# Attention and a feed-forward layer on one core: blocks of four pairs, grouped attention matmuls, three rooms for q and k, and one list scheduler for the whole program

## The chip, the core and the metric

The kernel runs on one core of a Trainium2 chip. Its time is the device time of one execution in microseconds (us), and the median of several runs is compared. The engines of the core work side by side: TensorE (PE in the profile) multiplies matrices, VectorE (DVE), ScalarE (ACT) and GpSimd (POOL) work on elements, and SyncE (SP) issues the DMA transfers. PEld is PE's loading of the stationary operand.

## The reference, cut to what matters

Attention runs inside chunks of 64 tokens, 8 heads of 64 columns; its output, as 4608 rows of 512 columns, goes through two linear layers with a squared ReLU between them.

```python
scores = scale * np.matmul(q_c, k_c.transpose(0, 1, 2, 4, 3))   # chunks of 64
attn = np.exp(scores - np.max(scores, axis=-1, keepdims=True))
attn = attn / (np.sum(attn, axis=-1, keepdims=True) + 1e-09)
out = np.matmul(attn, v_c)
x = out.transpose(0, 2, 1, 3).reshape(4608, 512)
h = x @ w_in                      # 512 -> 2048
g = np.maximum(h, 0.0) ** 2
return g @ w_out                  # 2048 -> 512
```

## The kernel before

Two chunks are a **pair** of 128 tokens; there are 36. Pairs are gathered into **blocks**, `blocks = [4] + [3] * 10 + [2]`. A block goes through the feed-forward part in 16 steps `f`, each for 128 of the 2048 middle columns. A step multiplies into `h` (`mm_in`, L623: a 128x128 piece of `w_in` stands in the array and the tokens of the block move through it, so a matmul has 128 columns for each pair of the block) and later out of `g` into `o` (`mm_out`, L667: the 128 tokens of one pair stand in the array and 512 columns of `w_out` move). The `o` sums stay in PSUM for all 16 steps, one bank for each pair of the block out of four; `outs` of a step come `LAG = 2` steps behind its `ins`.

Each fp32 operand is split into a high part and the remainder, both in the format in which PE multiplies; a product is three matmuls (high-high, high-low, low-high). A step thus has 12 `h` matmuls, and 3 `o` matmuls for each pair. Between them `Step` does ReLU (L634, ACT), the square (L638 on DVE from block 2 on, L640 on ACT ahead of that), the high part of `g` (L647, ACT) and the low part (L650, DVE).

Attention of the first eight pairs (`Pair`) runs in and ahead of block 0. The other 28 are worked as 56 **units** of four heads, each one slot of the stream behind the other: `stack_qk` transposes and splits q and k (DVE, ACT, and DMAs from one half of the partitions to the other), `s2` makes the scores (L353, four matmuls of 256 columns) and their softmax up to the exponential, `norm` divides (POOL, L390), `s3` transposes the result (L403, two of 128 columns) and stacks it as `pst` (L417, L419, L421), `s4` multiplies with v (L437, four of 256 columns) and writes the tokens `x` of a later block. The raw q and k have tiles of their own, the transposed ones too, and the low part of q has another.

What sets the order: in block 0 a planner (`Plan`) lists all engines' work by costs written into it and issues it in that order. From block 1 on only PE's order is written by hand: `merge` spreads the units' steps one by one, evenly, between the matmuls of the block. The other engines are ordered by the framework's scheduler, with `Step.act` and the stores ahead by a priority. `store` (L680) copies an `o` bank to one of two `ob` tiles (L677 on DVE, L679 on ACT) and issues its DMA.

Of the kernel before, what the change touches and what calls it, by code (L numbers as in the profile page):

```python
# [10 lines left out]
F32 = mybir.dt.float32  # L11
# [9 lines left out]
def kernel(  # L21
# [20 lines left out]
    nc = tc.nc  # L42
# [19 lines left out]
    PRIO = 300  # L62
    blocks = [4] + [3] * 10 + [2]
    LAG = 2
    HEAD = 1
    REST = 0
# [10 lines left out]
    NN = sum(blocks[:2]) + 1  # L77
# [12 lines left out]
    raw = ctx.enter_context(tc.tile_pool(name="raw", bufs=1))  # L90

# [18 lines left out]
    def open_late():  # L110

        early.close()
        pool = ctx.enter_context(tc.tile_pool(name="late", bufs=2))
        late["pool"] = pool
        late["q"] = pool.tile([P, H, 2, CH], F32R, name="qst", tag="qst", bufs=1)
        late["p"] = pool.tile([P, 2, HP, 2, 2, CH], F32R, name="pst", tag="pst", bufs=1)
        load_v(NN)
# [97 lines left out]
    ust = [dict() for _ in units]  # L215
# [27 lines left out]
    def load_qk(pair):  # L243


        pairs[pair] = {}
        for nm, src in (("q", q), ("k", k)):
            t = raw.tile([P, H, IH, 32], F32, name=f"{nm}_raw{pair}", tag=f"{nm}_raw")
            pairs[pair][nm] = t
            for c in range(2):  # L250
                bb, n0 = divmod(2 * pair + c, NCH)
                for dh in range(DH):
                    r0 = c * D + dh * 32
                    for ih in range(IH):
                        i0 = n0 * CH + ih * 32
                        s = src[bb, :, i0:i0 + 32, dh * 32:(dh + 1) * 32]
                        nc.sync.dma_start(out=t[r0:r0 + 32, :, ih, :], in_=s.rearrange("h i d -> i h d"))  # L257

    def load_v(pair):


        if pair < NN:
            for c in range(2):
                bb, n0 = divmod(2 * pair + c, NCH)
                for h2, r in enumerate(halves):
                    s = v[bb, h2:H:2, n0 * CH:(n0 + 1) * CH, :]
                    nc.sync.dma_start(  # L267
                        out=vbd[slot_of(pair)][r, :, c, h2, :], in_=s.rearrange("h i d -> i h d")
                    )
            return  # L270
        pairs[pair]["v"] = []
        for c in range(2):
            t = late["pool"].tile([P, H, D], F32, name=f"v_raw{pair}_{c}", tag="v_raw")
            pairs[pair]["v"].append(t)
            bb, n0 = divmod(2 * pair + c, NCH)
            s = v[bb, :, n0 * CH:(n0 + 1) * CH, :].rearrange("h i d -> i h d")
            for r in halves:
                nc.sync.dma_start(out=t[r], in_=s)

    def transpose_pair(pair):  # L280

        for nm in "qk":
            t = late["pool"].tile([P, H, CH], F32, name=f"{nm}t{pair}", tag=f"{nm}t", bufs=1)
            nc.vector.transpose(
                t.rearrange("p h i -> p (h i)"), pairs[pair][nm].rearrange("p h a d -> p (h a d)")
            )
            pairs[pair][nm] = t
        if pair + 1 < NPAIR:
            load_qk(pair + 1)

    def s1(u):
        b, pair, j, hq = units[u]
        if hq == 0:
            yield lambda: transpose_pair(pair)
            yield lambda: stack_qk(pair)

    def stack_qk(pair):

        qt, kt = pairs[pair]["q"], pairs[pair]["k"]
        kst = late["k"]
        qst = late["q"]
        low = late["pool"].tile([P, H, CH], F32R, name=f"ql{pair}", tag="kk", bufs=1)
        for c, (own, oth) in enumerate(other):
            nc.scalar.copy(qst[own, :, c], qt[own])  # L306
        for c, (own, oth) in enumerate(other):
            nc.vector.tensor_tensor(low[own], qt[own], qst.bitcast(F32)[own, :, c], op=ALU.subtract)
        for c, (own, oth) in enumerate(other):
            nc.sync.dma_start(out=qst.bitcast(F32)[oth, :, c], in_=low.bitcast(F32)[own])  # L310
        for c, (own, oth) in enumerate(other):
            nc.scalar.copy(kst[own, 0, c], kt[own])  # L312
        for c, (own, oth) in enumerate(other):
            nc.sync.dma_start(out=kst.bitcast(F32)[oth, 0, c], in_=kst.bitcast(F32)[own, 0, c])
        for c, (own, oth) in enumerate(other):
            nc.vector.tensor_tensor(
                kst[own, 1, c], kt[own], kst.bitcast(F32)[own, 0, c], op=ALU.subtract
            )

    def split_v(u):  # L320
        yield lambda: stack_v(u)

    def stack_v(u):


        b, pair, j, hq = units[u]
        vs = late["pool"].tile([P, 2, HP, 2, D], F32R, name=f"vs{u}", tag="vs")
        ust[u]["v"] = vs
        for c, t in enumerate(pairs[pair]["v"]):
            vr = t[:, hq * HQ:(hq + 1) * HQ].rearrange("p (a b) d -> p a b d", b=2)  # L330
            nc.scalar.copy(vs[:, c], vr)  # L331
            for h2, r in enumerate(halves):
                dst = (r, slice(None), 1 - h2)
                nc.gpsimd.tensor_tensor(  # L334
                    vs[:, c][dst], vr[dst], vs.bitcast(F32)[:, c][dst], op=ALU.subtract
                )
        if hq == NQ - 1 and pair + 1 < NPAIR:
            load_v(pair + 1)

    def s2(u):  # L340


        st = ust[u]
        b, pair, j, hq = units[u]

        def mm2(h):
            if h % 2 == 0:
                st.setdefault("sc", []).append(
                    bank(("at", next(turn_at) % 2), [P, 2, 2, 2, CH], f"sc{u}_{h}")
                )  # L350
            ps = st["sc"][-1][:, h % 2]
            hh = hq * HQ + h
            nc.tensor.matmul(  # L353
                ps.rearrange("p w c j -> p (w c j)"), late["q"][:, hh].rearrange("p c i -> p (c i)"), late["k"][:, :, :, hh],
                start=True, stop=True,
            )

        def half(h):
            if h == 0:
                st["e"] = late["pool"].tile([P, HQ, CH], F32, name=f"e{u}", tag="e", bufs=2)  # L360
            ps, e = st["sc"][h // 2], st["e"][:, h:h + 2]
            for c, r in enumerate(halves):
                nc.scalar.copy(e[r], ps[r, :, 1, c])  # L363
            for c, r in enumerate(halves):
                nc.vector.tensor_tensor(e[r], ps[r, :, 0, c], e[r], op=ALU.add)  # L365

        def rest():
            e = st["e"]
            m = att.tile([P, HQ, 1], F32, name=f"m{u}", tag="m", bufs=2)
            z = att.tile([P, HQ, 1], F32, name=f"z{u}", tag="z", bufs=2)  # L370
            nc.vector.tensor_reduce(m, e, axis=AX.X, op=ALU.max)
            nc.vector.tensor_tensor(e, e, m.broadcast_to([P, HQ, CH]), op=ALU.subtract)
            nc.scalar.activation(e, e, AF.Exp, scale=QSCALE)
            st["e"] = (e, z)

        for h in range(HQ):
            yield lambda h=h: mm2(h)
            if h % 2:
                yield lambda h=h: half(h - 1)
        yield rest  # L380

    def norm(u):
        st = ust[u]

        def f():
            e, z = st["e"]
            nc.vector.tensor_reduce(z, e, axis=AX.X, op=ALU.add)
            nc.vector.tensor_scalar_add(z, z, 1e-9)
            nc.vector.reciprocal(z, z)
            nc.gpsimd.tensor_tensor(e, e, z.broadcast_to([P, HQ, CH]), op=ALU.mult)  # L390
            st["p"] = e

        yield f

    def s3(u):

        st = ust[u]

        def tr(hp):
            if hp == 0:  # L400
                st["pt"] = bank(("at", next(turn_at) % 2), [P, HP, 2, CH], f"pt{u}")
            ps = st["pt"]
            nc.tensor.transpose(  # L403
                ps[:, hp].rearrange("p a b -> p (a b)"),
                st["p"][:, 2 * hp:2 * hp + 2].rearrange("p a b -> p (a b)"),
                ident,
            )

        for hp in range(HP):
            yield lambda hp=hp: tr(hp)  # L410

        def evac2():
            ps = st["pt"]
# [576 lines left out]
```

## Time and profile before

| | |
|---|---|
| time, median of 3 runs | 938.81 us (937.74 to 940.42) |
| profiled execution: span; the median above it | 936.7 us; 2.1 us |
| PE busy in it | 922.2 us (98%) |
| DVE, ACT, POOL busy | 691.0, 599.6, 211.1 us |
| h matmuls (L623) | 2304: 192 of 512 columns, 1920 of 384, 192 of 256 |
| o matmuls (L667) | 1728 of 512 columns |

The profiled execution's own time is that span and what lies around it outside the trace: the timed runs end 1.0 to 3.7 us above the span, the median 2.1 us above it. Busy time counts an engine's instructions; a busy PE can still be slower than it could be, since a matmul's time is what the next one waits for.

### The profile page before, as it was taken

The page shows a single profiled execution, that of the slowest core. Times are in us where ns is not written, and L with a number is a line of the kernel's source. Part 1 is how long each engine was busy: PE and PEld are TensorE (multiplying, and loading weights), DVE is VectorE, ACT ScalarE, POOL GpSimd, SP SyncE. Part 2 cuts the span into 40 slices and gives each one's busy share as a digit, 9 for nine tenths or more (in the row PEclk, how much of TensorE's full clock was granted, in tenths as well). Part 3 has the DMA queues.
Part 4 walks back from the last instruction along what each step waited for, and adds up shares of the span by engine and source line. Part 5 has one row for each costly group of instructions (what it writes and reads, how often), then busy time and mean ns, then how long its engine had stood idle before and what let it go on. Part 6 is the DMA issues. An engine that isn't in the chain of part 4 may idle for free.

```text
span 936.7 us, 16742 instructions
## 1 busy us (share of the span) xinstructions
PE 922.2 (98%) x5018; PEld 827.8 (88%) x5018; DVE 691.0 (74%) x1591; ACT 599.6 (64%) x1479; POOL 211.1 (23%) x351
## 2 busy tenths in 40 slices
PE   9899999999999999999999999999999999999998
PEld 8788888888899999999999999999999999998997
DVE  5999994678778877877877877877877877753332
ACT  5788876687666666766766766766766666653332
POOL 2000002043222233333322222333333222221000
PEclk9899999999999999999999999999999999999999
DMA  8946425445444543543433533444543442210000
GB/s 185 278 136 209 168 39 118 81 83 104 96 79 78 112 77 75 112 76 74 106 70 72 112 72 69 110 76 79 113 80 75 89 103 57 57 40 12 1 35 23
DMA packets 287193, 85.01 MB, mean 91 GB/s; under 512 B 268672, under 2 KB 276864, under 8 KB 287104
## 3 DMA queue, kind: packets, MB, share of 16 engines
q1 hardware_dynamic: 284992, 83.42, 40.7%
q8 instruction: 41, 0.67, 0.3%
q10 hardware_dynamic: 2112, 0.52, 0.3%
q14 instruction: 48, 0.39, 0.1%
HBM read 52.43 MB, written 9.44 MB: 66 GB/s over the span
## 4 chain that ended last, share of the span: by engine, by line
PE 90%; DVE 3%; ACT 2%; DMA 1%; SPq 1%; issue 1%; POOL 1%; ACTq 0%; DVEq 0%; POOLq 0%
PE h L623 41%; PE o L667 40%; PE sc L353 3%; PE xt L437 3%; PE pt L403 1%; PE xt L581 1%; PE sc L527 1%; DMA wiraw<-in_moe_w_in_dram 1%; SPq L257 0%; SPq L267 0%; ACT qst L306 0%; ACT kst L312 0%; POOL vbd L800 0%; DVE wia L177 0%; DMA kst<-kst 0%
## 5 line engine op out<-in xcount | busy, mean ns | idle before, releaser
L623 PE MATMUL h<-xh,wi 128*128 128x384 f32 (+2 forms) x1536 | 433.4, 339 | 0.2 <-DVE wi L198 0.2
L667 PE MATMUL o<-wo,gh 128*128 128x512 f32 x1152 | 372.0, 397 | 0.6 <-ACT ob L679 0.6
L623 PEld LDWEIGHTS h<-xh,wi 128*128 128x128 f32 x1536 | 274.9, 188 | 14.2 <-DVE wi L198 0.8
L623 PE MATMUL h<-xl,wi 128*128 128x384 f32 (+2 forms) x768 | 260.5, 339 | 0.2 <-DVE xl L594 0.2
L667 PEld LDWEIGHTS o<-wo,gh 128*128 128x128 f32 x1152 | 207.9, 188 | 33.7 <-ACT ob L679 1.0
L667 PE MATMUL o<-wo,gl 128*128 128x512 f32 x576 | 226.5, 393 | 0.0
L334 POOL TENSOR_TENSOR vs<-v_raw,vs 64x128 fp32r<-64x128 f32 x224 | 114.7, 512 | 238.8 <-ACT vs L331 218.8
L650 DVE TENSOR_TENSOR gl<-g,gh 128x384 fp32r<-128x384 f32 (+2 forms) x192 | 111.4, 580 | 68.8 <-ACT gh L647 64.8
L623 PEld LDWEIGHTS h<-xl,wi 128*128 128x128 f32 x768 | 144.6, 188 | 7.3 <-DVE xl L594 0.5
L634 ACT ACTIVATE g<-h 128x384 f32<-128x384 f32 (+2 forms) x192 | 94.5, 492 | 79.4 <-PE h L623 59.2
L647 ACT CAST gh<-g 128x384 fp32r<-128x384 f32 (+2 forms) x192 | 98.5, 513 | 71.0 <-PE o L667 53.3
L638 DVE TENSOR_TENSOR g<-g 128x384 f32<-128x384 f32 (+1 forms) x160 | 88.9, 556 | 64.1 <-ACT g L634 62.7
L667 PEld LDWEIGHTS o<-wo,gl 128*128 128x128 f32 x576 | 108.2, 188 | 20.7
L390 POOL TENSOR_TENSOR e<-e,z 128x256 f32<-128x256 f32 x56 | 45.3, 810 | 233.1 <-PE o L667 69.7
L365 DVE TENSOR_TENSOR e<-sc,e 64x128 f32<-64x128 f32 x224 | 64.7, 289 | 36.7 <-ACT e L363 31.4
L363 ACT COPY e<-sc 64x128 f32<-64x128 f32 x224 | 58.2, 260 | 43.1 <-PE sc L353 40.2
L451 DVE TENSOR_TENSOR x<-xt,x 64x128 f32<-64x128 f32 x224 | 64.6, 289 | 22.7 <-ACT x L449 18.5
L449 ACT COPY x<-xt 64x128 f32<-64x128 f32 x224 | 58.0, 259 | 35.2 <-PE xt L437 31.9
L353 PE MATMUL sc<-kst,qst 128*128 128x256 f32 x224 | 62.8, 281 | 2.0 <-DVE pst L421 1.2
L437 PE MATMUL xt<-pst,vs 128*128 128x256 f32 x224 | 62.6, 280 | 2.1 <-DMA pst<-pst 2.1
L457 POOL TENSOR_TENSOR xl<-x,xh 128x256 fp32r<-128x256 f32 x56 | 44.3, 790 | 59.5 <-ACT xh L456 57.1
L421 DVE TENSOR_TENSOR pst<-pt,pst 64x256 fp32r<-64x256 f32 x112 | 47.3, 422 | 10.9 <-ACT pst L417 6.9
(80 smaller groups left out, 912.4 us busy)
## 6 DMA issues: line engine op xcount, KB each, us to landing
v_raw<-in_v_dram SPq DMA_DIRECT2D x112, 128.0 KB, 3.3
out_dram<-ob SPq DMA_DIRECT2D x36, 256.0 KB, 2.1
wiraw<-in_moe_w_in_dram SPq DMA_DIRECT2D x16, 512.0 KB, 6.2
woraw<-in_moe_w_out_dram SPq DMA_DIRECT2D x16, 512.0 KB, 6.0
q_raw<-in_q_dram SPq DMA_DIRECT2D x224, 32.0 KB, 2.1
k_raw<-in_k_dram SPq DMA_DIRECT2D x224, 32.0 KB, 2.1
qst<-ql SPq DMA_DIRECT2D x56, 128.0 KB, 2.6
kst<-kst SPq DMA_DIRECT2D x56, 128.0 KB, 2.6
```

The costliest lines, as they stand in the source:

```text
L334: nc.gpsimd.tensor_tensor(vs[:, c][dst], vr[dst], vs.bitcast(F32)[:, c][dst], op=ALU.subtract)
L353: nc.tensor.matmul(ps.rearrange("p w c j -> p (w c j)"), late["q"][:, hh].rearrange("p c i -> p (c i)"), late["k"][:, :, :, hh], start=Tru ...
L363: nc.scalar.copy(e[r], ps[r, :, 1, c])
L365: nc.vector.tensor_tensor(e[r], ps[r, :, 0, c], e[r], op=ALU.add)
L437: nc.tensor.matmul(st["xt"][hp][:, c].rearrange("p w a q -> p (w a q)"), st["v"][:, c, hp].rearrange("p a d -> p (a d)"), late["p"][:, :, ...
L451: nc.vector.tensor_tensor(x[r, hp], ps[hp][r, :, 0, h2], x[r, hp], op=ALU.add)
L623: nc.tensor.matmul(self.h[:, :self.n], a[:, c], bb[:, c, :self.n], start=c == 0 and i == 0, stop=c == NCC - 1 and i == 2,)
L634: nc.scalar.activation(self.g, self.h[:, :self.n], AF.Relu)
L638: nc.vector.tensor_tensor(self.g, self.g, self.g, op=ALU.mult)
L647: nc.scalar.copy(self.gh[:, :self.n], self.g)
L650: nc.vector.tensor_tensor(self.gl[:, :self.n], self.g, self.gh.bitcast(F32)[:, :self.n], op=ALU.subtract)
L667: nc.tensor.matmul(acc[b, j], a[:, j * P:(j + 1) * P], bb, start=f == 0 and i == 0, stop=f == NF - 1 and i == 2,)
```

## The change

Blocks become nine of four pairs, so every `h` matmul has 512 columns. Each unit's work is cut into methods of one instruction each (class `Unit`), and the planner, which now knows a cost for every one of them, lists all engines of the whole program. PE's order stays fixed by a token that its work shares; the others go by what is ready first, then by a due time counted backwards. The attention of a unit no longer goes singly between matmuls but in three bunches in each slot, at 0, 0.31 and 0.62 of it. Raw and transposed q and k share a ring of three tiles, and the low part of q is written over the transposed q. The first late pair's raw q and k go into the two `ob` tiles, before any `ob` needs them. The square goes to DVE in even steps and to ACT in odd ones. The copy and the store of `o` are two operations now. The eight early pairs (`NN`) and all instructions of a unit stay.

```diff
-    blocks = [4] + [3] * 10 + [2]
+    blocks = [4] * 9
-    NN = sum(blocks[:2]) + 1
+    NN = sum(blocks[:2])
+        ring.extend(pool.tile([P, H * CH], F32, name=f"ring{n}", tag=f"ring{n}", bufs=1) for n in range(3))
...
+    def room(pair, n):
+        if pair == NN and n < 2:
+            return gp.tile([P, DM], F32, name=f"{'qk'[n]}_raw{pair}", tag="o")
+        return ring[(4 * (pair - NN) + n) % 3]
...
+            self.on_vector = b > 0 and f % 2 == 0
...
         def square(self):
-            if self.b > 1:
+            if self.on_vector:
...
-        HOP = 0.2
+        HOP = {PE: 0.27, DVE: 0.07, ACT: 0.07, POOL: 0.1, SP: 0.1}
...
+            for n in reversed(range(len(ops))):
+                engine, cost, _, _, size, rank = ops[n]
+                if size:
+                    cost += size / self.RATE + self.LATENCY
+                due[n] = min((due[x] - self.hop(n, x) for x in after[n]), default=self.END) - cost
+                if rank is not None:
+                    due[n] = rank
...
+                    key = (max(free.get(ops[n][0], 0.0), ready[n]), due[n], n)
...
+    SPOTS = (0.0, 0.31, 0.62)
+    LEAD = 0.06
...
+        def pe(cost, fn, reads, writes):
+            add(PE, cost, fn, reads, [*writes, "pe"])
...
+                if s.f == NF - 1:
+                    ob = ("ob", next(stores) % 2)
+                    add(DVE if j % 2 else ACT, TWO if j % 2 else ONE, lambda j=j: s.keep(j), [o], [ob])
+                    add(SP, ISSUE, lambda j=j: s.store(j), [ob], size=256 * KB)
...
+        def slot(t):
+            r = []
+            for at_, stages in zip(SPOTS, (((3, values),), ((2, turn), (2, split_v)), ((1, scores), (0, begin)))):
+                r.append((at_, [lambda st=st, un=unit[t - lag]: st(un) for lag, st in stages if NQ * NN <= t - lag < NU]))
+            return r
...
+        if not last:
+            n0 = NQ * first_pair[b + 1] + 3 if b > 1 else NQ * NN + 1
+            n1 = NQ * (first_pair[b + 1] + blocks[b + 1])
+            slots = [slot(t) for t in range(n0, n1 + 3)]
+        spread(ops, slots, LEAD if b == 1 else 0.0)
```

The first place is PE in the middle of a block, from step 5 to step 6 (`sc` are a unit's score matmuls, `xt` those with v). Before, they stand one at a time between matmuls of 384 and 512 columns:

```order
L623 MATMUL h_5_4708<-xh_3517,wi_768 128x384
L667 MATMUL o_0_4547<-wo_723,gh_3_4619 128x512 x2
L353 MATMUL sc_2_4737<-kst,qst 128x256
L667 MATMUL o_0_4547<-wo_723,gl_3_4620 128x512
L667 MATMUL o_1_4552<-wo_723,gh_3_4619 128x512 x2
L667 MATMUL o_1_4552<-wo_723,gl_3_4620 128x512
L353 MATMUL sc_2_4737<-kst,qst 128x256
L667 MATMUL o_2_4561<-wo_723,gh_3_4619 128x512 x2
L667 MATMUL o_2_4561<-wo_723,gl_3_4620 128x512
L623 MATMUL h_6_4758<-xh_3517,wi_821 128x384
```

Of the change, the same engine and steps:

```order
L598 MATMUL h_5_5458<-xh_4002,wi_778 128x512
L343 MATMUL sc_0_5478<-kst,qst 128x256 x2
L343 MATMUL sc_2_5481<-kst,qst 128x256 x2
L598 MATMUL h_5_5458<-xh_4002,wi_778 128x512
L598 MATMUL h_5_5458<-xl_4003,wi_778 128x512
L598 MATMUL h_5_5458<-xh_4002,wi_778 128x512
L635 MATMUL o_0_5279<-wo_738,gh_3_5417 128x512 x2
L635 MATMUL o_0_5279<-wo_738,gl_3_5418 128x512
L635 MATMUL o_1_5288<-wo_738,gh_3_5417 128x512 x2
L635 MATMUL o_1_5288<-wo_738,gl_3_5418 128x512
```

The four score matmuls moved together, the four with v do the same (eight rows further on), and all that stands between the bunches has 512 columns.

The second place is SP in block 0, where the raw q and k of the last two of the eight early pairs are loaded (`qk_raw`), with `vbd` the tile of v for one of them, which waits until PE is done with the one that it held. Before:

```order
L241 DMA qk_raw_504<-in_q_dram 128x4x64 x2
L241 DMA qk_raw_504<-in_k_dram 128x4x64 x2
L267 DMA vbd_89<-in_v_dram 64x4x64 x4
L146 DMA woraw_819<-in_moe_w_out_dram 128x1024
L144 DMA wiraw_824<-in_moe_w_in_dram 128x4x256
```

Of the change:

```order
L235 DMA qk_raw_501<-in_q_dram 128x4x64 x2
L235 DMA qk_raw_501<-in_k_dram 128x4x64 x2
L257 DMA q_raw_529<-in_q_dram 32x8x32 x8
L257 DMA k_raw_576<-in_k_dram 32x8x32 x8
L265 DMA vbd_86<-in_v_dram 64x4x64 x4
L141 DMA woraw_830<-in_moe_w_out_dram 128x1024
L139 DMA wiraw_834<-in_moe_w_in_dram 128x4x256
```

The 16 loads of the first late pair moved ahead of the `vbd` loads and of all weight loads behind them.

## Rows read from the trace of the kernel before

**Rows 1.** The page: span and busy time of each engine.

```profile
span 936.7 us, 16742 instructions
PE 922.2 (98%) x5018; PEld 827.8 (88%) x5018; DVE 691.0 (74%) x1591; ACT 599.6 (64%) x1479; POOL 211.1 (23%) x351
```

**Rows 2.** Windows: busy PE, PEld, DVE, ACT, POOL (instructions), PE clock, DMA, GB/s.

```profile
146.00:245.00 99.00, 94.40 (x496) 83.72 (x495) 68.42 (x163) 68.88 (x176) 25.45 (x45) 1.00 0.50 102
421.25:495.00 73.75, 73.75 (x397) 66.99 (x397) 58.27 (x141) 48.99 (x130) 21.83 (x36) 1.00 0.43 87
```

**Rows 3.** PE's waits, 146 us to the end: total us, times, longest.

```profile
PE xt L437 <- DMA pst<-pst: 2.1, 2, 1.3
PE pt L403 <- DVE x L451: 1.3, 1, 1.3
PE sc L353 <- DVE pst L421: 1.2, 3, 0.7
PE sc L353 <- DMA kst<-kst: 0.7, 1, 0.7
PE o L667 <- ACT ob L679: 0.6, 1, 0.6
```

**Rows 4.** Pieces of the chain: start, us, engine, tile, line, instructions.

```profile
49.81 2.72 PE h L623 x12
54.26 2.82 PE o L667 x12
59.80 2.04 PE o L667 x9
...
365.10 2.10 PE h L623 x12
413.62 2.08 PE o L667 x9
...
883.91 1.43 PE h L623 x12
```

**Rows 5.** Timeline of PE behind transposes of block 0.

```profile
40.54 0.39 PE L623 MATMUL h<-xl,wi 128*128 128x512 f32 x1
...
41.70 0.60 PE L503 MATMUL k<-ident,qk_raw 128*128 128x128 f32 x4
```

**Rows 6.** Groups of the page: busy us, mean ns, idle before them.

```profile
L390 POOL TENSOR_TENSOR e<-e,z 128x256 f32<-128x256 f32 x56 | 45.3, 810 | 233.1 <-PE o L667 69.7
L365 DVE TENSOR_TENSOR e<-sc,e 64x128 f32<-64x128 f32 x224 | 64.7, 289 | 36.7 <-ACT e L363 31.4
L363 ACT COPY e<-sc 64x128 f32<-64x128 f32 x224 | 58.2, 260 | 43.1 <-PE sc L353 40.2
```

**Rows 7.** DVE's groups by shape (columns as in rows 6).

```profile
L650 DVE TENSOR_TENSOR gl<-g,gh 128x384 fp32r<-128x384 f32 x160 | 93.6, 585 | 56.2 <-ACT gh L647 52.5 <-PE o L667 1.9
L638 DVE TENSOR_TENSOR g<-g 128x384 f32<-128x384 f32 x144 | 82.1, 570 | 44.7 <-ACT g L634 43.3
L650 DVE TENSOR_TENSOR gl<-g,gh 128x512 fp32r<-128x512 f32 x16 | 11.0, 686 | 0.6 <-ACT gh L647 0.3
```

**Rows 8.** SP's timeline in block 0, and eight loads later.

```profile
51.74 3.46 SPq L241 DMA_DIRECT2D qk_raw<-in_k_dram  x2
65.80 2.63 SPq L267 DMA_DIRECT2D vbd<-in_v_dram  x4
...
397.72 4.03 SPq L257 DMA_DIRECT2D k_raw<-in_k_dram  x8
```

**Rows 9.** The end's timeline, ACT's wait for ob, and the page's landing time.

```profile
932.47 0.59 ACT L679 COPY ob<-o 128x512 f32<-128x512 f32 x1 [1.86 <-PE o L667]
933.15 0.69 DVE L677 COPY ob<-o 128x512 f32<-128x512 f32 x1 [2.08 <-PE o L667]
ACT ob L679 <- DMA out_dram<-ob: 9.9, 11, 2.0
out_dram<-ob SPq DMA_DIRECT2D x36, 256.0 KB, 2.1
```

More of the change, by code (lines that the diff above doesn't have):

```diff
@@ L259, in load_v @@
-    def load_v(pair):
[L262 to L271, printed above, removed]
+    ring = []
+    def room(pair, n):
+        if pair == NN and n < 2:
+            return gp.tile([P, DM], F32, name=f"{'qk'[n]}_raw{pair}", tag="o")
+        return ring[(4 * (pair - NN) + n) % 3]
@@ new lines, in load_qk @@
+    def load_qk(pair, n, part):
+        src = (q, k)[n]
+        at = pairs.setdefault(pair, {})
+        if n not in at:
+            at[n] = room(pair, n)
+        t = at[n].rearrange("p (h a d) -> p h a d", h=H, a=IH)
+        c, dh, ih = part
+        bb, n0 = divmod(2 * pair + c, NCH)
+        r0 = c * D + dh * 32
+        i0 = n0 * CH + ih * 32
+        s = src[bb, :, i0:i0 + 32, dh * 32:(dh + 1) * 32]
+        nc.sync.dma_start(out=t[r0:r0 + 32, :, ih, :], in_=s.rearrange("h i d -> i h d"))
@@ L291, in s1 @@
[L291 to L315, printed above, removed]
+            for h2, r in enumerate(halves):
+                s = v[bb, h2:H:2, n0 * CH:(n0 + 1) * CH, :]
+                nc.sync.dma_start(
+                    out=vbd[slot_of(pair)][r, :, c, h2, :], in_=s.rearrange("h i d -> i h d")
+                )
@@ L340, in s2, with raw_v @@
[L340 to L346, printed above, removed]
-            if h % 2 == 0:
[L348 to L352, printed above, removed]
+                late["k"][own, 1, c], pairs[self.pair]["t", 1][own],
+                late["k"].bitcast(F32)[own, 0, c], op=ALU.subtract,
+            )
+        def raw_v(self, c):
+            return pairs[self.pair]["v", c][:, self.heads].rearrange("p (a b) d -> p a b d", b=2)
@@ new lines, in high_v, with low_v, score @@
+        def high_v(self, c):
+            if not c:
+                self.v = late["pool"].tile([P, 2, HP, 2, D], F32R, name=f"vs{self.u}", tag="vs")
+            nc.scalar.copy(self.v[:, c], self.raw_v(c))
+        def low_v(self, c, h2):
+            dst = (halves[h2], slice(None), 1 - h2)
+            nc.gpsimd.tensor_tensor(
+                self.v[:, c][dst], self.raw_v(c)[dst], self.v.bitcast(F32)[:, c][dst], op=ALU.subtract
+            )
+        def score(self, h, which):
+            if h % 2 == 0:
+                self.sc = bank(which, [P, 2, 2, 2, CH], f"sc{self.u}_{h}")
+            ps = self.sc[:, h % 2]
+            hh = self.hq * HQ + h
@@ L380, in s2 @@
[L380 to L402, printed above, removed]
+                ps.rearrange("p w c j -> p (w c j)"), late["q"][:, hh].rearrange("p c i -> p (c i)"),
@@ new lines, in score, with take, join @@
+                late["k"][:, :, :, hh], start=True, stop=True,
+            )
+            if h % 2:
+                self.done = getattr(self, "done", {})
+                self.done[h // 2] = self.sc
+        def take(self, part, c):
+            if not part and not c:
+                self.e = late["pool"].tile([P, HQ, CH], F32, name=f"e{self.u}", tag="e", bufs=2)
+            r = halves[c]
+            nc.scalar.copy(self.e[r, 2 * part:2 * part + 2], self.done[part][r, :, 1, c])
+        def join(self, part, c):
+            r = halves[c]
+            e = self.e[r, 2 * part:2 * part + 2]
+            nc.vector.tensor_tensor(e, self.done[part][r, :, 0, c], e, op=ALU.add)
@@ L425, in s3, with high_p @@
-        yield evac2
-    def s4(u):
-        st = ust[u]
-        b, pair, j, hq = units[u]
-        def mm2(hp, c):
-            if c == 0:
-                st.setdefault("xt", []).append(
-                    bank(("at", next(turn_at) % 2), [P, 2, 2, 2, CH], f"xt{u}_{hp}")
-                )
+                self.pt[:, hp].rearrange("p a b -> p (a b)"),
+                self.e[:, 2 * hp:2 * hp + 2].rearrange("p a b -> p (a b)"), ident,
+            )
+        def high_p(self, h2):
+            own, _ = other[h2]
+            nc.scalar.copy(late["p"][own, 0, :, :, h2], self.pt[own])
@@ new lines, in send_p, with low_p, value @@
+        def send_p(self, h2):
+            own, oth = other[h2]
+            f = late["p"].bitcast(F32)
+            nc.sync.dma_start(out=f[oth, 0, :, :, h2], in_=f[own, 0, :, :, h2])
+        def low_p(self, h2):
+            own, _ = other[h2]
+            nc.vector.tensor_tensor(
+                late["p"][own, 1, :, :, h2], self.pt[own],
+                late["p"].bitcast(F32)[own, 0, :, :, h2], op=ALU.subtract,
+            )
+        def value(self, hp, c, which):
+            if not c:
+                if not hp:
+                    self.xt = []
+                self.xt.append(bank(which, [P, 2, 2, 2, CH], f"xt{self.u}_{hp}"))
@@ L459, in s4, with take_x, join_x @@
-        for hp in range(HP):
-            for c in range(2):
-                yield lambda hp=hp, c=c: mm2(hp, c)
-            yield lambda hp=hp: evac(hp)
+        def take_x(self, hp, h2):
+            if not hp and not h2:
+                self.x = late["pool"].tile([P, HP, 2, CH], F32, name=f"x{self.u}", tag="x", bufs=1)
+            r = halves[h2]
+            nc.scalar.copy(self.x[r, hp], self.xt[hp][r, :, 1, h2])
+        def join_x(self, hp, h2):
+            r = halves[h2]
+            x = self.x[r, hp]
+            nc.vector.tensor_tensor(x, self.xt[hp][r, :, 0, h2], x, op=ALU.add)
@@ L464, in x_of, with place @@
+        def place(self, part):
+            xh, xl = x_of(self.b)
+            dst = (slice(None), slice(self.hq * HP, (self.hq + 1) * HP), slice(self.j * P, (self.j + 1) * P))
+            src = self.x.rearrange("p a c i -> p a (c i)")
+            if part == 0:
+                nc.scalar.copy(xh[dst], src)
+            else:
+                nc.gpsimd.tensor_tensor(xl[dst], src, xh.bitcast(F32)[dst], op=ALU.subtract)
     def x_of(b):
@@ L767, in run @@
                 t, _, n = best
-                engine, cost, _, _, size, _ = ops[n]
-                free[engine] = t + cost
-                end[n] = t + cost
+                engine, cost, fn, _, size, _ = ops[n]
+                end = free[engine] = t + cost
                 if size:
-                    queue = max(queue, t + cost) + size / self.RATE
-                    end[n] = queue + self.LATENCY
+                    queue = max(queue, end) + size / self.RATE
+                    end = queue + self.LATENCY
+                if loads and loads[-1] == n:
+                    loads.pop()
                 order.append((t, n))
-                left.remove(n)
+                open_.remove(n)
+                for x in after[n]:
+                    ready[x] = max(ready[x], end + self.hop(n, x))
+                    waits[x] -= 1
+                    if not waits[x]:
+                        open_.add(x)
+            assert len(order) == len(ops)
             for _, n in sorted(order):
@@ new lines, with spread @@
+    unit = [Unit(u) for u in range(NU)]
+    def spread(ops, slots, start):
+        todo = [((start + (1 - start) * (s + at) / len(slots)) * len(ops), x) for s, groups in enumerate(slots) for at, x in groups]
+        for n, op in enumerate(ops):
+            while todo and todo[0][0] <= n:
+                for x in todo.pop(0)[1]:
+                    x()
+            op()
+        for _, xs in todo:
+            for x in xs:
+                x()
+    with tc.manual_schedule(engines={PE, DVE, ACT, SP, POOL}):
+        program()
```

419 lines of the change are left out of this document (234 added, 185 removed).

## The prediction

> **What bounds the kernel now.** I read the page first: PE is busy 922.2 of 936.7 us, DVE 691.0, ACT 599.6 [rows 1]. That a busy PE is also the one that is waited for must come from a stretch, so the windows came next. In 421 to 495 us, which is exactly one block of three pairs, PE is busy 73.75 of 73.75 us; DVE has 58.27 (79%), ACT 48.99 (66%) [rows 2]. In 146 to 245 us, where the units begin, PE is busy 94.40 of 99.00, so 4.6 us are lost there. The list of PE's waits confirms that there is little else: after 146 us they sum to 5.9 us, five kinds [rows 3]. So the kernel is bounded by the spacing of PE's own matmuls, and the question is what one costs in each shape.
>
> The pieces of the chain give that [rows 4]. Twelve h matmuls of 512 columns take 2.72 us, 226.7 ns each; of 384 columns 2.10 us, 175 ns; of 256 columns 1.43 us, 119 ns. Nine o matmuls, 512 columns, take 2.04 us in block 0 when nothing of another shape stands ahead of them (226.7 ns) and 2.08 us later (231.1 ns), where matmuls of 384 and 256 columns stand among them. In block 0, where all feed-forward matmuls have 512 columns, one piece of twelve behind attention takes 2.82 us. The timeline shows the same directly behind transposes: from 40.54 to 41.70 us five matmuls start, 232 ns each (the first row and the one behind the fifth) [rows 5]. I read this as: a foreign shape disturbs the spacing of the some ten matmuls behind it by about 4.4 ns each (231.1 less 226.7).
>
> A check: a block of three is 192 x 0.175 + 144 x 0.2311 = 66.9 us of h and o; the remaining 6.85 us of 73.75 are six units, 1.14 us a unit on PE.
>
> **The change, part by part.**
>
> *Blocks of four.* Before: h is 192 x 0.2267 + 1920 x 0.175 + 192 x 0.119 = 402.4 us. After: 1728 x 0.2267 = 391.7. The columns are the same in sum; 576 fixed costs go. By the rows that fixed cost is 13 to 15 ns (226.7 less 512 columns at 2.4 GHz is 13.4; 175 less 160 is 15; the granted clock is 1.00 in these windows [rows 2], its level of 2.4 GHz). o before: 192 x 0.2267 in block 0 and 1536 x 0.2311 after it, 398.5 us; after, undisturbed, 391.7. Together 800.9 to 783.4: **-17.5 us**.
>
> On this point a rule speaks against the change. The Trainium skill, "TensorE: Matmul & The Clock Gate", section "Wait — 56ns, not 53.3ns?", gives a fixed cost of about 2.5 ns for a warm matmul; by it 576 fewer matmuls are worth 1.4 us, not the 10.7 us of h. The trace differs, with 13 to 15 ns at three widths, and I go by the trace.
>
> *Attention in bunches.* Each of 56 units has three bunches: 168 places where the shape changes, in blocks 1 to 7. With ten disturbed matmuls behind each, 1680 of the 2688 there cost 4.4 ns more: **+7.4 us**. Nothing in the trace shows these groups between 512-wide matmuls alone. The lower bound is 0 (the 2.04 us piece), the upper one all 3072 matmuls of blocks 1 to 8, 13.5 us (the 2.08 us piece). I take the middle because attention stands nearest to it. The attention matmuls are the same in number and shape, 1.14 us a unit: 0.
>
> *Waits.* A slot in blocks 2 to 7 is (384 x 0.229 + 8 x 1.14) / 8 = 12.1 us. Scores stand at 0.62 of a slot, the transpose at 0.31 of the next: 0.69 x 12.1 = 8.3 us. What must happen between is, by the groups, the second part's copies (2 x 0.26) and adds (2 x 0.289), four softmax operations on DVE and ACT (an estimate: 256 elements a row where the adds have 128 in 0.289 us, so between 0.29 and 0.58, 0.42 each), small ones, and 0.81 us on POOL [rows 6]: some 4.5 us, 5 with hops. The product with v has the same 8.3 us, against about 4.6 for the copy, the transfer (2.1 us as the stores' landing [rows 9]) and the subtraction. For q and k of a new pair: one slot of 12.1 us, against two transposes (like other 512-wide DVE work, 0.69 [rows 7]), copies of 0.59, subtractions of 0.69 and a transfer, about 8. Block 1 is tightest: ten slots, 6.0 us for the first distance, and its first unit cannot be ahead. Of the 5.9 us of waits now, most in the first slots, I keep 2.5 (0.6 at the start as in the largest single o wait [rows 3], 0.7 for the first unit, 1.2 for what I don't see): **-3.4 us**; bounds 0 and 10 us.
>
> *Other engines.* DVE for a block of four: attention is (58.27 - 16 x (0.585 + 0.570)) / 3 = 13.3 us a pair [rows 2, 7]; 4 x 13.3 + 16 low parts at 0.686 + 8 squares at about 0.69 = 69.5 of 97.2 us, 72% instead of 79%. ACT at most 4/3 x 48.99 + 8 x 0.59 = 70 us, 72%. Neither becomes the bound. Cost: 0.
>
> *Early loads of the first late pair.* 16 loads at 0.5 us (eight took 4.03 us) stand ahead of a `vbd` load. SP issued nothing from 55.20 to 65.80 us there, since that load waits for PE [rows 8]; the 8.1 us fit. Cost 0; without the cover up to 8 us for the weights behind them.
>
> *Four o banks.* All four are now filled at a block's end, with two `ob` tiles: the third and fourth copies wait until the first stores have landed. Copy 0.59 and landing 2.1 us and the third copy's 0.59 set the third bank free about 3.7 us after the first bank's last matmul, and it is needed 6.1 us after that (three more o groups of 0.68, 12 h matmuls, two o groups). Some 2.4 us of slack: 0. At the end of the program nothing hides it. Before, the last copy starts with the end of the last matmul (933.15 [rows 9]). After, the fourth copy needs the second's tile: that sum ends 1.36 us ahead of the last, 0.69 for its copy and 2.1 to land, so it starts about 1.4 us past the last matmul: **+1.4 us**.
>
> *Sum.* -17.5 + 7.4 - 3.4 + 1.4 = -12.1: span 936.7 to 924.6; with the 2.1 us between that span and the median, **926.7 us**.
>
> **The rivals.**
>
> *The gain is eaten.* All matmuls behind block 0 are disturbed (+13.5 instead of +7.4), the waits stay at 5.9, and the copies of four banks make each of eight boundaries wait 0.6 us (4.2 more than the one now). For it: ACT already waited 9.9 us in 11 times for an `ob` tile [rows 9]. Against: the slack above. 936.7 - 17.5 + 13.5 + 1.4 + 4.2 = 938.3, so 940.4 us.
>
> *Slower: the bunch is not ready.* PE's order is fixed, a bunch stands at a fixed place, and all of PE stands behind it if its operands are late, be it q and k through the ring or the softmax, whose operations the planner places on each engine by its own costs. It would be seen at `sc`, `pt` and `xt`. Price: the 4.6 us lost in 146 to 245 us, eight slots of 12.3 us, are 0.57 us a slot; for 56 units 32 us, so 956 us. It decides from 0.31 us a unit: (941.6 - 924.2) / 56, with 924.2 the forecast without waits. For it: those eight slots. Against: in 421 to 495 us no unit waits at all, and the distances above leave 3 us. The Trainium skill, "TensorE: Matmul & The Clock Gate", in its table of the engine, has the queues of ScalarE, VectorE and GpSimd as strictly first in, first out; by it one late operation at a queue's head holds up the others whether or not they are ready, as ACT's waits for `ob` do here.
>
> *The fixed cost is not what it seems.* If wide h matmuls next to others cost as the disturbed o did, and only 2.5 ns a matmul are saved, the h gain is 1.4 us instead of 10.7: 926.7 + 9.3 = 936.0 us. Three widths in rows speak against it.
>
> **How the numbers follow.** Forecast 0.73, its own range 921.5 (no disturbance, less 5.2) to 932; fixed cost 0.05; gain eaten 0.07; bunches late 0.15. A measurement of this kernel tells about 0.3% (2.8 us) from no change, so 936.0 to 941.6 is no change. Faster 0.78 (forecast and fixed cost, which is at the edge), same 0.07, slower 0.15. The range is 921.5 to 937.5: it leaves out the gain eaten and the late bunches.
>
> **What would show it.** Right: one group of 1728 h matmuls of 512 columns; pieces of twelve at 2.72 to 2.77 us; a block of 97.2 us with PE busy throughout; PE's waits after 146 us near 2.5 us; DVE at 72% in a block; SP's 16 loads ended before PE releases the `vbd` load; the last DVE copy 1.4 us past the last matmul. Wrong: twelve at 2.77 or more in all of the blocks (gain eaten), or `sc`, `pt`, `xt` at the head of PE's waits, by 0.3 us or more a unit.

## The result, and the profile after

The changed kernel takes 930.34 us (median of 4 runs, 929.43 to 931.06) against 938.61 for the kernel before in the same series; the ratio is 0.9907 with a 95% interval of 0.9893 to 0.9921. It is faster by 8.3 us where 12.1 were forecast, and the time lies in the range.

The page of the changed kernel, for [rows 1]:

```profile
span 928.1 us, 15185 instructions
PE 912.3 (98%) x4442; PEld 759.6 (82%) x4442; DVE 654.9 (71%) x1452; ACT 614.3 (66%) x1426; POOL 217.8 (23%) x351
```

PE is still the engine that all wait for, with 10 us less to do. The run of this trace took 929.85 us, 1.75 more than its span. The windows (columns as in [rows 2]) show first the stretch from 140 to 250 us, which holds block 1, then one block of four:

```profile
140.00:250.00 110.00, 105.19 (x493) 85.88 (x493) 87.89 (x204) 80.21 (x200) 38.22 (x61) 0.98 0.50 99
342.45:439.70 97.25, 97.25 (x466) 81.10 (x465) 72.64 (x171) 68.04 (x171) 29.93 (x48) 1.00 0.43 87
```

The block of four takes 97.25 us with PE busy throughout; 97.2 were forecast. In the first stretch PE stands idle for 110.00 - 105.19 = 4.81 us, and the granted clock is 0.98. The same stretch of the kernel before:

```profile
140.00:250.00 110.00, 105.40 (x548) 93.06 (x547) 76.23 (x179) 76.63 (x193) 28.87 (x49) 1.00 0.49 99
```

That is 4.60 us idle at a full clock. So the loss at the start of the late units, which the forecast more than halved, is as large as it was. PE's waits from 146 us on, for [rows 3]:

```profile
PE sc L343 <- DMA qst<-ring: 2.3, 1, 2.3
PE sc L343 <- DVE gl L625: 1.1, 1, 1.1
PE sc L343 <- DMA kst<-kst: 0.5, 1, 0.5
PE pt L390 <- DVE x L432: 0.4, 1, 0.4
PE xt L417 <- ACT kst L308: 0.4, 1, 0.4
PE o L635 <- DVE ob L643: 0.3, 1, 0.3
PE sc L343 <- DVE pst L406: 0.2, 1, 0.2
```

They sum to 5.2 us, and 4.1 of them stand at the first score matmul of a unit (`sc`), for its stacked q and k (`qst`, `kst`) or behind DVE. The largest is worth following on PE's timeline:

```profile
190.73 0.39 PE L635 MATMUL o<-wo,gl 128*128 128x512 f32 x1
193.41 1.09 PE L343 MATMUL sc<-kst,qst 128*128 128x256 f32 x4 [2.30 <-DMA qst<-ring]
194.30 0.63 PE L598 MATMUL h<-xh,wi 128*128 128x512 f32 x1
194.73 0.63 PE L598 MATMUL h<-xl,wi 128*128 128x512 f32 x1
```

No matmul starts between 190.73 and 193.41 us. Behind that gap the next ones stand 0.43 us apart, which is 512 columns at the clock's lower level of 1.2 GHz, and only after some 3 us are they back at 0.23. In the window from 193.40 to 197.00 us the granted clock is 0.53, from 197.00 to 200.00 it is 1.00. What was late is seen on DVE and on SP, in the same stretch:

```profile
185.03 0.68 DVE L298 TENSOR_TENSOR ring<-ring,qst 64x512 fp32r<-64x512 f32 x1
186.48 0.69 DVE L298 TENSOR_TENSOR ring<-ring,qst 64x512 fp32r<-64x512 f32 x1
...
183.92 2.69 SPq L282 DMA_DIRECT2D v_raw<-in_v_dram  x4
186.65 1.11 SPq L257 DMA_DIRECT2D ring<-in_q_dram  x2
187.88 0.52 SPq L313 DMA_DIRECT2D kst<-kst  x1
188.49 0.63 SPq L304 DMA_DIRECT2D qst<-ring  x1
189.21 0.60 SPq L313 DMA_DIRECT2D kst<-kst  x1
189.87 0.58 SPq L257 DMA_DIRECT2D ring<-in_q_dram  x1
190.54 0.59 SPq L304 DMA_DIRECT2D qst<-ring  x1
```

SP issues almost without a pause, some 0.6 us each. The low parts of q that the two `qst` transfers carry were done on DVE at 185.7 and 187.2 us; the transfers leave at 188.49 and 190.54, since loads of v and of the next q, and transfers of k (`kst`), stand ahead of them. The pieces of the chain, for [rows 4], one of them a block of eight slots behind another:

```profile
194.50 3.94 PE h L598 x12
366.76 2.73 PE o L635 x12
418.60 2.75 PE h L598 x12
464.02 2.73 PE o L635 x12
827.45 2.72 PE o L635 x12
```

Twelve wide matmuls take 2.72 us in the last block, where no attention stands between them, and 2.73 to 2.75 elsewhere; 3.94 us is the stretch at the low clock, 1.2 us more. At the end of the program, for [rows 9]:

```profile
922.57 0.39 PE L635 MATMUL o<-wo,gl 128*128 128x512 f32 x1
923.70 0.58 ACT L643 COPY ob<-o 128x512 f32<-128x512 f32 x1 [2.15 <-DMA out_dram<-ob]
924.51 0.69 DVE L643 COPY ob<-o 128x512 f32<-128x512 f32 x1 [2.18 <-DMA out_dram<-ob]
```

The last two copies wait for stores. The last one starts 1.55 us after the end of the last matmul (922.96), where before it started with that end.

### The profile page after: what moved, and what is told of

It is laid out like the page before. It is cut to its first block, busy times and chain, and to the rows that moved or that the text cites. A ratio compares the mean times of both kernels' runs of the same rounds, so it can differ in the third digit from the quotient of the medians.

```text
span 928.1 us, 15185 instructions
## 1 busy us (share of the span) xinstructions
PE 912.3 (98%) x4442; PEld 759.6 (82%) x4442; DVE 654.9 (71%) x1452; ACT 614.3 (66%) x1426; POOL 217.8 (23%) x351
## 4 chain that ended last, share of the span: by engine, by line
PE 84%; DVE 4%; ACT 4%; DMA 3%; SPq 3%; issue 1%; POOL 1%; DVEq 0%; ACTq 0%; POOLq 0%
PE h L598 38%; PE o L635 37%; PE xt L417 3%; PE sc L343 3%; SPq L257 1%; DMA v_raw<-in_v_dram 1%; PE xt L561 1%; PE pt L390 1%; PE sc L507 1%; DMA wiraw<-in_moe_w_in_dram 1%; SPq L265 1%; SPq L282 0%; DMA pst<-pst 0%; DVE gl L625 0%; ACT gh L622 0%
## 5 line engine op out<-in xcount | busy, mean ns | idle before, releaser
L598 PE MATMUL h<-xh,wi 128*128 128x512 f32 x1152 | 391.0, 394 | 0.5 <-DVE wi L193 0.5
L598 PEld LDWEIGHTS h<-xh,wi 128*128 128x128 f32 x1152 | 217.3, 189 | 44.0 <-DVE wi L193 1.4
L598 PE MATMUL h<-xl,wi 128*128 128x512 f32 x576 | 225.9, 392 | 0.2 <-DVE xl L574 0.2
L625 DVE TENSOR_TENSOR gl<-g,gh 128x512 fp32r<-128x512 f32 x144 | 101.8, 707 | 71.0 <-ACT gh L622 67.2
L609 ACT ACTIVATE g<-h 128x512 f32<-128x512 f32 x144 | 86.2, 598 | 73.3 <-PE h L598 62.0
L622 ACT CAST gh<-g 128x512 fp32r<-128x512 f32 x144 | 89.4, 621 | 64.6 <-PE o L635 50.8
L598 PEld LDWEIGHTS h<-xl,wi 128*128 128x128 f32 x576 | 109.0, 189 | 19.2 <-DVE xl L574 0.5
L613 DVE TENSOR_TENSOR g<-g 128x512 f32<-128x512 f32 x64 | 53.7, 840 | 52.3 <-ACT g L609 49.9
L397 ACT CAST pst<-pt 64x256 fp32r<-64x256 f32 x112 | 40.8, 364 | 25.9 <-PE pt L390 24.3
L615 ACT ACTIVATE g<-g 128x512 f32<-128x512 f32 x80 | 50.6, 633 | 2.3
```

Source lines behind the costliest of these rows:

```text
L598: nc.tensor.matmul(self.h[:, :self.n], a[:, c], bb[:, c, :self.n], start=c == 0 and i == 0, stop=c == NCC - 1 and i == 2,)
L609: nc.scalar.activation(self.g, self.h[:, :self.n], AF.Relu)
L613: nc.vector.tensor_tensor(self.g, self.g, self.g, op=ALU.mult)
L615: nc.scalar.activation(self.g, self.g, AF.Square)
L622: nc.scalar.copy(self.gh[:, :self.n], self.g)
L625: nc.vector.tensor_tensor(self.gl[:, :self.n], self.g, self.gh.bitcast(F32)[:, :self.n], op=ALU.subtract)
```

## The experiments

All times are medians beside the kernel before on the same chip (938.6 to 939.6 us). "Idle" is the window from 140 to 250 us less PE's busy time in it, in the run's profile.

**Old widths under the new scheduler.**

```diff
-    blocks = [4] * 9
+    blocks = [4, 4] + [3] * 8 + [4]
```

> The changed kernel with blocks of 4, 4, then eight of 3, then 4; scheduler, bunches and rooms stay. Width theory (a narrower h matmul saves less than its columns, 175 ns for 384 against 226.7 for 512): the stretch of blocks 2 to 9, 28 pairs less four, takes 8 x 73.5 to 73.75 = 588 to 590 us where six blocks of four took 583.5, so 4.5 to 6.5 us more there. Rival (only about 2.5 ns a matmul is fixed, the gain comes from the scheduler): 384 matmuls more cost 1 us there. Beside it, block 1 now has six units to work in eight slots instead of eight in ten; the theory that block 1's slots are too short for its queues expects its waits of 5.2 us to fall below 2.5; the rival that these waits belong to the first units expects about 5 still. The whole: 928 to 936 us.

935.63 us (933.31 to 937.78); ratio to before 0.9963 (0.9948 to 0.9978). One piece of its chain and the same one a block of three later, and its window:

```profile
380.97 2.09 PE o L635 x9
455.17 2.09 PE o L635 x9
140.00:250.00 110.00, 110.00 (x530) 92.52 (x529) 81.26 (x184) 76.38 (x185) 35.07 (x54) 1.00 0.47 94
```

A block of three takes 74.20 us, against the 73.75 of [rows 2] in another profile. Against 97.02 us for a block of four (the run with two more tiles, same chip), 24 pairs cost 8 x 74.20 - 6 x 97.02 = 11.5 us more. The width theory had the sign and too little (4.5 to 6.5); its rival, 1 us, is refuted. Added up from each matmul's start to the next one's in the two profiles, 8.5 of the 11.5 us lie on h, 0.5 on o and 2.4 on attention: 384 more h matmuls cost 22 ns each. And block 1, which has six units to work here in eight slots, instead of eight in ten, loses nothing: 0.00 us idle. Less the 4.8 us idle and the 1.7 us of low clock that the changed kernel loses there, the 11.5 us are 5.0, and the whole is 5.3 us slower than the changed kernel on its chip. It is still 3.5 us faster than the kernel before; how much of that is the scheduler, and how much the bunches and the first and last blocks, was not parted.

**Attention singly.** The stages yield after each matmul and the slots are laid out finer:

```diff
-            for at_, stages in zip(SPOTS, (((3, values),), ((2, turn), (2, split_v)), ((1, scores), (0, begin)))):
+            for at_, n, lag, stage in ((0.0, 4, 3, values), (0.31, 2, 2, turn), (0.36, 1, 2, split_v),
+                                       (0.47, 4, 1, scores), (0.62, 1, 0, begin)):
+                ...
+                        r.append((at_ + 0.05 * i, [lambda x=x: next(x, None)]))
```

> The changed kernel with the ten attention matmuls of a unit standing singly between groups of three 512-wide ones instead of in three bunches. Disturbance theory (each change of shape disturbs some ten matmuls by 4.4 ns): all 48 matmuls of a slot are now disturbed, where 30 were: a block of four takes 97.25 + 8 x 18 x 0.0044 = 97.9 us and the whole is about 4 us slower, 934. Rival (only the count of attention matmuls matters, not their grouping): 97.2 us a block and 930 us. Rival (the disturbance is paid once for each single one): a block above 98.5 us and the whole above 938.

934.81 us (932.35 to 936.52). A piece and the same one a block later:

```profile
381.85 2.73 PE o L635 x12
479.51 2.73 PE o L635 x12
```

97.66 us a block, 0.64 more than the 97.02 of the bunches on this chip, as the disturbance theory has it (0.63); six blocks make 3.9 us. Both rivals fall. That the numbers meet so closely is luck: from start to start, the 384 wide matmuls take 89.93 us instead of 88.37 here, 1.56 more, and the attention matmuls 0.91 less. Its idle time is 6.7 us, as in the unedited kernel's second profile (below).

**Two more tiles at the end.**

```diff
+            if self.b == len(blocks) - 1 and j > 1:
+                o = ring[j - 2]
+            else:
+                o = gp.tile([P, DM], F32, name=f"ob{self.b}_{j}", tag="o")
...
```

> The changed kernel, but the last block's third and fourth sums are copied to two tiles of the ring, which are free by then, instead of the two ob tiles. If the ob tiles hold up the end: the last copy starts with the end of the last matmul, the end comes about 1.5 us earlier, 928.8. Rival (four stores on SP and the transfers bound the end anyway): less than 0.7 us.

928.00 us (925.51 to 929.13). The end, and two pieces a block of four apart:

```profile
389.57 2.73 PE o L635 x12
486.59 2.73 PE o L635 x12
...
919.70 0.39 PE L635 MATMUL o<-wo,gl 128*128 128x512 f32 x1
920.13 0.69 DVE L646 COPY ring<-o 128x512 f32<-128x512 f32 x1 [0.67 <-PE o L635]
```

The last copy starts with the end of the last matmul again. From the start of the last matmul to the end of the span it is 4.0 us (span 923.7) against 5.5 in the changed kernel (928.1 - 922.57): 1.5 us, as expected. The rest of the 2.3 us between the medians lies within the spread (below).

**Six tries at block 1's loss.** Loads held back behind transfers that are soon ready:

```diff
+                    hold = 1.5 if ops[n][0] == SP and ops[n][1] in (0.5, 0.55) else 0.0
-                    key = (max(free.get(ops[n][0], 0.0), ready[n]), due[n], n)
+                    key = (max(free.get(ops[n][0], 0.0), ready[n]) + hold, due[n], n)
...
```

> The changed kernel, but the planner holds back the loads of q, k and v by 1.5 us of its own time, so that a transfer between halves of the partitions (qst, kst, pst) that is ready soon goes ahead of them on SP. If block 1 waits because urgent transfers stand behind loads in SP's queue: the wait of sc for qst (2.3 us) and the fall of the clock behind it (about 1.5 us) go, some 4 us, 926 to 927. Rival (block 1 waits because ACT and DVE are late for its short slots): the waits move to another unit, within 1 us of 930.

930.63 us (929.05 to 930.88), 6.7 us idle. The wait for `qst` is gone, and PE waits for the transposes' operands instead (`pt` for DVE, POOL and ACT, 6.3 us). With these loads held back the loss moved; it did not go.

Shorter slots, from `LEAD = 0.06` to `LEAD = 0.16`:

> The changed kernel, but block 1's ten slots begin at 0.16 of the block instead of 0.06, so that each is 84 instead of 94 hundredths of a tenth of the block. Density theory (block 1 loses time because its slots of 9.4 us are shorter than the chains and queues of a unit can follow; with eight slots it lost nothing): slots of 8.4 us, 1 us less for each of the nine behind the first, and 4 to 9 us more of late matmuls in block 1; the other blocks unchanged; 934 to 939. Rival (the loss belongs to the start of the units, not to the length of the slots): block 1 as long as before within 1.5 us, 930.

930.61 us (928.81 to 931.18), 5.2 us idle. The density theory falls in this form: 1 us less a slot costs nothing that can be told from the spread.

All squares on DVE, `self.on_vector = b > 0`:

> The changed kernel with every square from block 1 on put on DVE, none on ACT. The step of the prediction that other engines' work costs nothing where PE has no waits: DVE rises to 80% in a block of four, which stays at 97.0 to 97.3 us. If block 1's waits come from DVE's queue, they grow by 2 us or more there; if from ACT's, they fall by as much; if from SP's, they stay within 1 us. The whole 928 to 933.

927.69 us (927.56 to 928.91), 3.5 us idle; blocks of four stay at 97.0 us, so more work on DVE costs nothing there. And all of them on ACT, `self.on_vector = False`:

> The changed kernel with every square from block 1 on put on ACT, none on DVE; the opposite of the run with all of them on DVE, which took 927.7. If ACT's queue is what makes units late in block 1: 2 to 5 us more lost there, 932 to 935, and blocks of four behind it unchanged at 97.0 to 97.3. Rival (any move between the two only reshuffles the order): within 1.5 us of 930.

930.03 us (927.55 to 931.93), 4.8 us idle. ACT's queue is not shown to be the cause: the opposite edit cost nothing.

The loads of v on POOL's queue (`nc.gpsimd.dma_start` for `nc.sync.dma_start`, cost 0.9 on POOL):

> The changed kernel with the loads of v for the late pairs issued by POOL instead of SP. If block 1's waits come from SP's queue (some 2.6 us of issue for the four v loads of a pair, 81% of a pair of slots there in sum): about 2 to 4 us less lost in block 1, 927. Rival (ACT's and DVE's order in the short slots): block 1 within 1 us of 109 us; 930.

929.13 us (927.63 to 931.63), 4.5 us idle: no effect that can be told. v for each unit in tiles of half the size, two in turn:

```diff
-                at["v", c] = late["pool"].tile([P, H, D], F32, name=f"v_raw{self.pair}_{c}", tag="v_raw")
+                at["v", self.hq, c] = late["pool"].tile([P, HQ, D], F32, name=f"v_raw{self.u}_{c}", tag=f"v_raw{c}")
...
-                fetch_v(un.pair + 1)
+            fetch_v(un.u + 2)
```

> The changed kernel with v loaded for each unit into its own half-size tile, two of them in turn, instead of for a pair into one tile: eight loads a pair instead of four, but a load need not wait until the unit ahead is done with its v. If what holds block 1 up is that a late v load stands at the head of SP's and ACT's queues: 2 to 4 us less in block 1, 927. Rival (SP's number of issues): 2 us more lost there, 932; rival (length of the slots whatever the loads): within 1 us of 930.

934.33 us (931.77 to 935.73), 7.8 us idle: worse, as the rival on SP's count had it, though the edit also halves each transfer and moves the time at which a load may start, so that the count alone is not shown to be the cause.

**The planner's costs set to the trace.**

```diff
-            add(DVE if s.on_vector else ACT, 0.7 if s.on_vector else ONE, s.square, [], ["g"])
+            add(DVE if s.on_vector else ACT, 0.84 if s.on_vector else 0.63, s.square, [], ["g"])
...
-                        add(SP, 0.55, lambda c=c, r=r: un.load_v(c, r), ["late"], [("vraw", c, r)], size=128 * KB)
+                        add(SP, 0.67, lambda c=c, r=r: un.load_v(c, r), ["late"], [("vraw", c, r)], size=128 * KB)
...
-            add(POOL, 0.65, un.norm, [z], every)
+            add(POOL, 0.83, un.norm, [z], every)
```

> The changed kernel, but from block 1 on the planner's costs are set to what the trace shows (squares on DVE 0.84 us instead of 0.70, ACT's 512-wide operations 0.63 for 0.60, DVE's 0.71 for 0.66, SP's issues 0.55 to 0.67 for 0.50 to 0.62, POOL's 0.58 and 0.83 for 0.52 and 0.65, a transfer's latency 2.4 for 1.8). The kernel's own plan holds waits of PE in block 1 for under 1 us; the trace has 7. If block 1 loses time because the order on the queues was made for a timetable that the chip does not keep: 3 us or more less lost in block 1, 926 to 927. Rival (ten units' work in block 1 is too much for the queues in any order): within 1.5 us of 930.

925.51 us (924.24 to 926.84); ratio 0.9862 (0.9844 to 0.9880), clear of the changed kernel's first series (0.9893 to 0.9921), but not of its second (0.9874, 0.9858 to 0.9891, below). Its window and the larger of its two waits of PE:

```profile
140.00:250.00 110.00, 108.18 (x513) 88.01 (x512) 91.38 (x210) 82.86 (x208) 41.32 (x65) 1.00 0.53 104
PE sc L343 <- DMA kst<-kst: 1.1, 2, 0.8
```

1.8 us idle, less than any other run with eight units in block 1, and the granted clock stays at 1.00. It points to the timetable as the cause, in one profile of an execution of 924.41 us; the other three took 924.24, 926.62 and 926.84.

**Together, and the changed kernel once more.**

> The three edits that gained alone, together: the planner's costs as measured (4.8 us), two ring tiles for the last two sums (2.3 us) and all squares from block 1 on on DVE (2.7 us). The end and the order are apart, so the tail's 1.5 to 2.3 us come on top; costs and squares both act on block 1's late units, where 3 us are left with the costs alone, so they do not add fully: 922 to 924. Rival (squares on DVE add nothing once the plan is true, or bring DVE's queue in): 924 to 925.5.

925.55 us (923.56 to 925.99); ratio 0.9857 (0.9842 to 0.9872), 4.4 us idle. It is far below the kernel before and 1.8 us below the changed kernel on the same chip, which is little more than the tail's 1.5 us. It is no faster than the costs alone: the squares on DVE added nothing, as the rival had it, or took some back (the spread hides which), and the little idle time of the run with costs alone did not come again.

> The changed kernel once more, with nothing edited, on the chip of the run beside it, to see how far block 1 and the steady blocks of one program move from run to run: 929 to 931; blocks 3 to 6 at 97.0 or 97.25 us; block 1 at 107.5 to 110 us.

927.35 us (926.50 to 931.34), lower than the first series: the intervals of the two series of one program, 0.9858 to 0.9891 and 0.9893 to 0.9921, do not meet. Its profile (929.6 us span) is of the longest execution, 931.34 us:

```profile
140.00:250.00 110.00, 103.27 (x478) 84.26 (x477) 84.68 (x197) 77.34 (x194) 37.46 (x60) 0.97 0.48 96
```

6.7 us idle, against 4.8 in the first trace of the same program, with blocks of four at 97.0 us instead of 97.25. A third profile belongs beside these two: the run with two more tiles has the unedited kernel's order on every engine and on SP until the last copies, so its block 1 is the unedited one. Its window, and the first ReLU of block 1 and of block 2 in the first profile, in that run and in this one:

```profile
140.00:250.00 110.00, 105.42 (x501) 85.93 (x500) 89.34 (x206) 81.43 (x203) 38.43 (x61) 1.00 0.50 100
143.64 0.60 ACT L609 ACTIVATE g<-h 128x512 f32<-128x512 f32 x1 [0.91 <-PE h L598]
253.39 0.60 ACT L609 ACTIVATE g<-h 128x512 f32<-128x512 f32 x1
...
144.14 0.60 ACT L609 ACTIVATE g<-h 128x512 f32<-128x512 f32 x1 [0.91 <-PE h L598]
252.19 0.60 ACT L609 ACTIVATE g<-h 128x512 f32<-128x512 f32 x1
...
143.61 0.60 ACT L609 ACTIVATE g<-h 128x512 f32<-128x512 f32 x1 [0.91 <-PE h L598]
256.31 0.60 ACT L609 ACTIVATE g<-h 128x512 f32<-128x512 f32 x1
```

With one order, block 1 takes 109.75, 108.05 and 112.70 us, with 4.8, 4.6 and 6.7 us idle. In the run with true costs it takes 105.41 (144.21 to 249.62), 2.6 less than the shortest of these, in the one profile there is; with all squares on DVE it takes 107.85, 0.2 less than the shortest. The start moves too: block 0's first ReLU comes between 40.57 and 42.98 us in the profiles. So idle times from 4.6 to 6.7 us say nothing of an edit, nor do medians from 927.4 to 930.3.

## Why the prediction was right, and where it was off

**Blocks of four and bunches** (-17.5 and +7.4): right in sum. A block took 97.25 us for 97.2. Two small errors cancel in it: from start to start the 384 wide matmuls take 88.6 us, where the sum had 88.1, and attention 8.65, where it had 9.1. The run with single matmuls shows that the bunches save what the forecast gave them, in sum. The run with the old widths shows that the gain is the width: under the new scheduler too, a pair costs more in blocks of three, and most of that lies on h, 8.5 us for 384 matmuls where the prediction's 175 and 226.7 ns make 7.6. The rival "the fixed cost is not what it seems" falls with it. The low end of the forecast's own range takes 5.2 us off for no disturbance, where the sum had 7.4; nothing hangs on it.

**Waits** (-3.4): the step that was mis-sized. "Of the 5.9 us of waits now, most in the first slots, I keep 2.5." The listed waits went to 5.2 us, and 1.2 us for the twelve matmuls at the low clock and about 0.5 for the scores ahead of them (1.09 us, where four take 0.64 at the full clock) come on top: about +1.0 instead of -3.4. With it the sum is -7.7, against -8.6 of the spans and -8.3 of the medians. I had compared how far apart the stages stand with how long a chain lasts alone. For a new pair's q and k the distance was a slot of 12.1 us, that of blocks 2 to 7; block 1's ten slots are some 9 us each. In a steady block SP begins the last of their transfers 5.4 us after the scores ahead of them (438.37 to 443.81 us), which with 2.5 us to land (the median of `kst`, where the forecast had 2.1) makes about the 8 us forecast. In block 1 it was 9.3 us (181.27 to 190.54), 3.4 of them from the end of the second low part of q to the start of its transfer; with 2.8 us to land (the median of `qst`) that is the 12.1 us after which the next scores began. The rival "the bunch is not ready" named the mechanism and `sc` as its place; it holds in block 1 alone, as blocks 3 to 6 have PE busy without a gap.

What makes block 1 lose is shown in part. Six units in longer slots instead of eight: nothing is lost; the two were not parted. A plan with the trace's durations: 1.8 us in one profile, but 4.4 with the squares moved as well. Moving one queue's work, in either direction: no effect beyond the spread, or another wait. Shorter slots did not make it worse, so the length of the slots alone is not shown to be it. That q and k share three tiles was not tried as a cause; the kernel before, with tiles of their own, lost 4.60 us in the same stretch. Why block 1 loses, and how much of the gain with true costs is their order and how much the spread, stays open; true costs with the two ring tiles and without the squares were not run.

**Other engines** (0): right, though DVE's share is 72.64 of 97.25, 75% for 72%, in part since eight squares of 0.84 us instead of 0.69 make 1.2 of the 3.1 us more; with all of them on DVE the steady block is the same.

**Early loads** (0): right, with nothing to spare. SP took 9.8 us for them instead of 8.1, and the `vbd` load behind them left at 65.62 where before it left at 65.80 [rows 8]:

```profile
55.66 5.92 SPq L257 DMA_DIRECT2D q_raw<-in_q_dram  x8
61.62 3.90 SPq L257 DMA_DIRECT2D k_raw<-in_k_dram  x8
65.62 2.62 SPq L265 DMA_DIRECT2D vbd<-in_v_dram  x4
```

**Four o banks** (0): one wait of 0.3 us. **The tail** (+1.4): 1.5, the difference of the two ends above, and two free tiles take it back.

## What to carry to other kernels

A list scheduler that fixes the order on every queue rests on its durations, and here some were a fifth too short. Planning again with durations from a trace of the scheduled kernel is worth a try; that it helps is not shown here. What is shown is how far a stretch that is full of waits moves by itself: with one order on every queue, block 1 took 108.05 to 112.70 us. Before a small edit there is credited, take the unedited kernel more than once, and see whether its profile is of a short or of a long execution. And when a change does not take away a known stall, keep the stall in the forecast, and compare each chain with the shortest slot that it must fit: a chain that fits its distance in the steady blocks says little about the queues in a stretch where several units start.

## What was not expected of the hardware

In this kernel a square on DVE in place, `g<-g`, takes longer in the mean than the subtraction of the same shape:

```profile
L625 DVE TENSOR_TENSOR gl<-g,gh 128x512 fp32r<-128x512 f32 x144 | 101.8, 707 | 71.0 <-ACT gh L622 67.2
L613 DVE TENSOR_TENSOR g<-g 128x512 f32<-128x512 f32 x64 | 53.7, 840 | 52.3 <-ACT g L609 49.9
```

The operation itself is not slower: the shortest of either take 647 and 650 ns, in the run with all squares on DVE the means are 769 and 750, and before they were 570 and 585 for 384 columns [rows 7]. What lengthens single ones was not tried.

After one idle stretch of 2.30 us on a PE that had been busy, the matmuls ran at 1.2 GHz for about 3 us. So a late transfer cost 4 us where its wait is listed with 2.3. In the window from 140 to 250 us the same happened behind waits of 1.9 us (all squares on ACT), 2.6 (v for each unit) and 2.9 (the changed kernel once more); in the other profiles no wait there is longer than 1.7, and the granted clock is 1.00. The longest of the waits of the first case and of the last of the others:

```profile
PE sc L343 <- DMA kst<-kst: 3.4, 3, 1.9
PE xt L417 <- DMA pst<-pst: 1.7, 1, 1.7
```

This is part of why one order gives block 1 three lengths: no fall of the clock in 108.05 us, one in 109.75, and a longer one in 112.70 (0.53 granted from 193.00 to 200.25 us).

And one program had blocks of 97.25 us in one profile and of 97.0 in another, with the same matmuls in the same order; what sets it was not tried.
